# Two channels in one state matmul, and the kernel's spectrum in one part instead of two

## The chip, the cores and the metric

The kernel runs on one core of a Trainium2 chip. A core has five engines that run side by side, each with its own instruction stream: TensorE (PE in the profile; its weight loads are shown as PEld), VectorE (DVE), ScalarE (ACT), GpSimd (POOL) and SyncE (SP). TensorE multiplies a stationary operand, loaded beforehand ("weights"), by a moving one and writes to PSUM; VectorE or ScalarE copy results from PSUM to SBUF, which the text calls an eviction. DMA queues are fed by SP, POOL and ACT. The metric is the time of one execution in microseconds of device time. Three runs of the kernel before gave 386.98, 386.78 and 383.81 us, with the median at 386.78.

## The reference, cut to what matters

Two branches read the same input x (2048 positions, 640 channels) and are mixed by a gate for each position.

```python
g = sigmoid((x * gate_w).sum(-1, keepdims=True))
# A: attention, 32 heads of 20, each position sees 8 positions: itself and 2, 4, ..., 14 back
qkv = x @ wqkv
logits = einsum("bhsd,bhswd->bhsw", q, kg) * Dh ** -0.5      # masked before the start
a = einsum("bhsw,bhswd->bhsd", softmax(logits), vg) @ wo
# B: a long convolution; channel d has 192 complex states n
logdA = dt[:, None] * (A_re + 1j * A_im)
P = exp(logdA[:, :, None] * l[None, None, :])                # l = 0 .. 2047, rounded to bf16
K = einsum("dn,dnl,dn->dl", Cc, P, dt[:, None] * Bc).real    # 640 kernels of 2048 taps
y = irfft(rfft(x, 4096) * rfft(K, 4096))[:2048] + x * Dskip
out = g * a + (1 - g) * y
```

Since l is rounded to bf16, only 641 different values of l occur. The kernel uses this: it computes K at l = 0 and at 20 x 32 values l = 8i + m (i below 32, m out of a list of 20), and takes the spectrum of K by one matrix that has the repeats summed in it.

## The kernel before, in words

**Branch A.** The input is turned (turn), multiplied by wqkv in four pieces of 512 positions (late, L278), and then eight chunks of 256 positions run through products q*k (prod, DVE, L336), a sum over the head (lg, PE, L342), softmax (max, neg, exp, sum, at), a trip through DRAM that spreads the weights (ast, asb, SP), products with the values (pv, DVE, L405), their sums (gat, PE, L411), the eviction (oT), and the multiplication by wo (wo, PE, L429), whose eviction multiplies by g (ga, L438). A chunk's result goes to the DRAM tensor gaS (SP, L448).

**Branch B, the taps.** The 640 channels run in ten chunks of 64. `KGen.plan` gives each chunk 18 argument matmul tasks (arg, PE, L759), whose results ScalarE turns into sines and exponentials (act, L771 and L773). For each of three groups u of states VectorE forms products (pq, three instructions, L790 to L792), and PE sums over the states (kmm, L808). One matmul of a kmm task belongs to one channel: its stationary operand is 32 columns wide (the i), its moving operand 20 columns (the m), and four channels lie side by side in the four column strips of the array. There are 64 such matmuls in a task and four tasks in a chunk (one for u = 0, two for u = 1, one for u = 2), so 2560 matmuls in all. The sums of one chunk lie in one PSUM buffer (slot kb); VectorE evicts it into E (fin, L868).

**Branch B, the spectrum of the taps.** `KSpec.part` works on two parts: the first six chunks (48 columns of 4 channels, 192 in all) and the last four (128 columns). When a part's last chunk is done, PE turns E (move, L885), the result is evicted (kev), and for each of 16 pieces k (8 frequency blocks, real and imaginary) a piece of the spectrum matrix W of 320 KB is fetched (wl, SP, three buffers) and multiplied (ks, L918). The first part does a piece in two tasks, the second in one. Results are evicted to the tile sk (ske, L458 or L460). W is therefore read twice.

**Branch B, the convolution.** The input is fetched a second time (rows), its first transform is 20 tasks (fu, L1029), evicted to Bu (fue). `Conv.spectra` then does, for each part and each of the 8 frequency blocks, the second transform (fp, L1064), its eviction (fe), and six VectorE instructions that multiply by the spectrum (ta, tc, Y, L1091 to L1097). `Conv.inverse` does 20 steps of two tasks (inv, L1122), each evicted to C (cp): twelve belong to the first part and need only its products, eight to the second part. `Conv.tail` does 11 groups of last matmuls (yp, L1164), mixes them with g * a, read from gaS into gaF (gaf, L1144), and stores the result (L1191).

**What sets the order.** Every piece of work is a task with a number, in the order in which `Plan.add` is called. The list SEQ gives the order in which all tasks are emitted and, where a task may run on several engines, the one it runs on (A, D, S, G). Each engine runs its tasks in that order, so a task that waits holds up all that stand behind it on its engine. Buffers are handed over by slots: a task acquires a slot and another releases it. PSUM is divided into two buffers of two banks (slot ar: turns, arg, move, fu, fp), two of one bank (tb: late, gat, wo and ks), one bank for lg and one for kb. For the last eight inverse tasks and the tail, all eight banks become four buffers cy.

Of the kernel before, what the change touches and what calls it, by code (L numbers as in the profile page):

```python
# [50 lines left out]
15A 14S 25 18G 13S 27 16A 20S 12S 23 3A 35 26 30 4A 0A 36A 37A 11S 9S 7S 40 31 8G 10A 24 28 32 29 39 38 49 52 53 44 108 109A 110 111A 106 107A 112 41 113D 104 105A 125  # L51
131 17S 1G 2G 19G 100 103S 101 6G 102S 5S 1158G 252G 124 33 43 126D 132D 54 45 46 135 145 82 136D 146A 63 47 48 50 60D 61D 62 166 127 21 167A 55 128A 137 122 83 138A 123A
141 22A 142A 174 175D 118 51 170 156 116 171A 160 157A 119A 161A 117A 149 150A 120 164 71 165A 68 57 69 70 65 77D 78 79 66 56 1147G 84 73 151 114 139 152A 58 140A 74 177
179 178A 180A 185 88A 186A 183 121A 184A 181 153 86 87 260 89 76 85 90A 182A 64 42 72 59 75 67 187S 91D 92 154A 115A 93 261 133 129 134D 34 95 80 130A 97 98 94 96 81 99
551 253 143 144A 209 262 264 263 265 147 254 210A 148A 162 266 268 267 269 255 270 163A 172 217 256 173A 257 296 218D 271 272 553 555 211 215 554 556 557 558 559 560 273
552 831 561 562 563 564 565 567 566 598 258S 836 597 547G 176 548G 298 212D 216D 274 297 569 568 570 571 299 573 572 574 575 576 300 301 577 302 168 303 579 304 305 169D
578 580 581 582 583 585 584 586 188 587 599 213 588 600 601 603 602 604 306 589 189D 591 214D 275 1156S 155G 331S 276 841 549 550 259G 332 590 605 307 607 592 606 608 609
610 611 612 192 613 158 614 615 617 616 618 593 643 644 219G 619 620 621 623 622 624 625 627 626 628 629 631 630 632 633 634 645 646 594 193D 277 1157 635 280 159D 595
637 596 647 649 648 650 241 651 653 652 654 278 655 657 283 334 279D 636 640 656 658 659 660 661 662 663 664 665 666 667 668 308 638 669 198 639 671 199D 242D 309 670 672
673 674 675 676 310 206 677 679 678 680 641 295G 689 690 311 312 735 736 333 691 681 642 683 336 284 693 682 335 692 694 207A 695 697 696 698 281 282D 285D 338 686 699  # L60
337 701 684 700 702 703 704 200 705 286 707 339 706 708 709 710 287D 201D 288 711 713 289A 712 714 204 715 717 716 685 719 687 718 720 340 368 313 688 727 721 723 205A
722 724 194 725 737 726 738 195A 243 739 741 728 740 742 743 744 244A 290 745 747 341 746 748 292 749 751 750 752 729 732 342 291D 293A 730 731 753 755 754 756 314 757
759 343 315A 758 760 344 208 202 190 761 763 345 316 319 370 191D 762 764 765 767 766 768 346 317 773 318A 769 770 733 369 771 371 782 781 294 347 912 348 911 783 320 772
785 784 786 321A 203A 734 774 372 374 373 787 789 788 790 375 249 376 404 377 791 793 250A 792 794 247 378 379 248A 380 775 795 322 381 324 797 776 796 798 799 800 323D
382 325A 326 801 803 777 802 805 804 405 807 806 808 327A 328 809 811 810 812 329A 196 813 815 220 778 406 408 349 352 814 816 197A 817 913 818 914 407 779 409 915 917
221A 916 350 919 353 410 780 918 920 351A 354A 921 923 411 922 924 245 925 927 926 928 246A 224 929 931 355 412 819 440 367G 820 413 356 821 442 414 824 930 932 225A 933
935 934 936 357A 222 937 939 223A 226 228 415 938 940 251G 957 383 384 330 958 385 941 943 227A 416 942 944 822 823 229A 358 417 945 947 946 948 359A 825 230 418 959 961
360 441 443 231A 960 962 361A 963 965 238 964 966 239A 826 949 444 446 445 448 967 969 362 232 968 970 363A 233A 388 827 447 449 364 828A 365A 450 829 830A 234 451 235A
452 971 973 386 950 236 972 974 387A 975 977 453 403G 240 1148G 976 978 1003 419 1004 420 366 389 979 981 237A 980 982 951 476 391 954 454 478 390D 952 953 983 985 955
984 986 987 988 477 989 990 392 991 479 993 393A 394 992 994 395A 455 1005 1007 396 398 1006 1008 1009 1011 397A 1010 1012 399A 832 1013 1015 480 421 482 995 956 833D 481  # L70
400 1014 1016 1017 1019 1018 1020 483 996 1021 1023 1022 1024 997 1000 484 401A 422 1025 1027 998 999 1026 1028 423A 1029 1031 1030 1032 834 837 485 1001 835A 838A 424
427 1041 1002 1033 1035 839 1034 1036 840A 425 1037 1039 426A 428 842 1038 1040 1049 1051 1052 1149G 1150G 1151G 1152G 1153G 1154G 1155G 1050 456 439G 402 429D 486 430
843A 1053 1055 431A 1054 1056 487 432 434 433A 488 435A 1057 1059 1058 1060 844 436 489 845A 437A 1061 1063 1062 1064 1043 512 457 490 514 846 851 856 491 492 438 475G
1159G 460 1042 847 458 1044 1065 1067 848A 1066 1068 513 515 1045 1069 1071 459A 1070 1072 516 463 849 517 1073 1075 850A 461 464 1074 1076 462A 465A 1161 1162A 466 468
1077 1078 467A 469A 1046 518 520 1047 519 521 1079 1081 1080 1082 470 472 471A 473A 522 1087 1048 523 1083 1085 493 1084 1086 524 852 1163 1165 1088 525 494 1164A 853A
1166A 526 1167 1169 854 1168A 1170A 495A 1089 1092 1171 1173 1172A 857 1174A 1175 1177 858A 1176A 1178A 1160S 474 527 861 528 511G 496 499 497 855D 498A 529 1179 1180A
1181 500 1183 1090 1091 1182A 501D 1184A 1093 502 504 1201 1203 532 503D 505A 506 507A 508 509A 1202D 1204D 1205 1206 1208 1210 1209A 1211A 530 1215 1216A 859 1217 535
1207 531A 860D 1218A 866 510 871 1185 533 1186A 1222 862 1224 1223A 1225A 534D 1212 1094 863D 1213 1214 1219 536 1187 537A 538 540 539A 541A 542 544 543D 545A 1229 1230A
1188A 864 867 865D 1220 1221 868D 1189 1190A 1191 869 1231 872 1192A 870A 1226 1227 873D 1236 1232A 1237A 1193 1194A 546 876 881 874 877 1238 1195 878D 1239A 879 1197
1196D 1199 880D 1228 875A 1233 1234 1198A 1200A 882 884 883A 885D 1235 1097 1095 1096A 1098D 886 891 1357G 1358G 1359G 887 889 888A 1243 890D 1244A 1240 1245 1246A 1241  # L80
1242 892 894 893A 895A 1250 1251A 896 897 898A 899 900A 1247 1248 1249 901 906 902 904 903A 907 905A 908A 909 910D 1254 1099 1102 1105 1100 1101A 1252 1257 1253D 1258D
1103 1104A 1255 1256 1259 1260 1261 1108 1262 1106 1107A 1263A 1109 1110A 1264 1265 1266 1111 1297 1298 1299A 1114 1117 1112 1113A 1267 1268A 1272 1115 1277 1273A 1278A
1118 1116D 1269 1300 1301 1303 1304 1270 1271 1305D 1119A 1120 1123 1126 1302A 1121 1122A 1274 1275 1124 1282 1129 1132 1127 1125A 1283A 1306 1307 1309 1310 1130 1128A
1276 1279 1280 1281 1308A 1311A 1287 1133 1131D 1288A 1134A 1312 1313 1315 1316 1135 1138 1141 1136 1314A 1292 1139 1317A 1137D 1284 1285 1140D 1286 1289 1290 1293A 1318
1319 1321 1322 1144 1142 1145 1320A 1323A 1146A 1324 1325 1326A 1291 1327 1328 1329A 1330 1331 1332A 1143D 1294 1295 1296 1333 1334 1360G 1335D 1361G 1362G 1363G 1364G
1365G 1366G 1367G 1368G 1336 1337 1338A 1339 1340 1341D 1342 1343 1345 1346 1348 1349 1344A 1351 1347D 1350A 1352 1354 1353D 1355 1356A 1369 1370 1372 1373 1371 1374 1375
1376 1379 1384 1380 1377 1385 1381 1378 1382 1383 1386 1391 1394 1398 1387 1388 1389 1390 1392 1395 1393 1396 1397 1399 1400 1401 1402 1403 1405 1406 1404 1407 1408 1410
1411 1409
# [3 lines left out]
class Task:  # L92

    def __init__(self, idx, name, eng, fn, deps, after, acq, rel, table):
        self.idx, self.name, self.engs, self.fn, self.table = idx, name, eng, fn, table
        self.deps, self.after, self.acq, self.rel = [d for d in deps if d], [d for d in after if d], list(acq), list(rel)


class Plan:

    SLOTS = {"ar": 2, "tb": 2, "lg": 1, "kb": 1, "trg": 5, "exq": 5, "pq": 2, "qs": 2, "ks": 2, "vs": 1, "vw": 1, "vc": 2, "prod": 2,
             "at": 2, "asb": 2, "pv": 2, "oT": 1, "ga": 1, "pc": 6, "cy": 4, "yp": 4, "ot": 7, "tt": 4, "W": 3, "su": 3}
# [46 lines left out]
class Attn:  # L149
# [159 lines left out]
    def plan_core(self, pl, pvb, g_sb, ps):  # L309
# [12 lines left out]
        for sc in range(S // C):  # L322
# [10 lines left out]
            for e in range(5):  # L333
# [4 lines left out]
                def logits(_, e=e, b=b):  # L338
                    if e == 0:
                        b["lg"] = ps.tile([128, W, 64], F32, name="lg")  # L340
# [987 lines left out]
```

## Time and profile before

| what | us |
|---|---|
| median of three runs | 386.78 |
| the profiled execution: its own time | 386.59 |
| its span, first to last instruction | 384.8 |
| PE busy | 314.6 |
| DVE busy | 304.5 |
| ACT busy | 293.2 |
| first argument matmul (L759) starts | 66.3 |
| last argument matmul starts | 255.3 |
| last spectrum matmul (L918) ends | 356.2 |

The profile gives the busy time of each engine, the stretches in which it was idle and what ended them ("<-PE ar L759" is the matmul of line 759 that writes ar; "issue" is time in which the engine waited for nothing that the profile shows). A line of a helper stands for all its callers: L458 and L460 are the evictions by ScalarE and VectorE. The busy time of PE is counted from the start of each matmul to its modelled end, which overlaps the next one; a distance between two starts is therefore the better price.

### The profile page before, as it was taken

The page shows a single profiled execution, that of the slowest core. Times are in us where ns is not written, and L with a number is a line of the kernel's source. Part 1 is how long each engine was busy: PE and PEld are TensorE (multiplying, and loading weights), DVE is VectorE, ACT ScalarE, POOL GpSimd, SP SyncE. Part 2 cuts the span into 40 slices and gives each one's busy share as a digit, 9 for nine tenths or more (in the row PEclk, how much of TensorE's full clock was granted, in tenths as well). Part 3 has the DMA queues.
Part 4 walks back from the last instruction along what each step waited for, and adds up shares of the span by engine and source line. Part 5 has one row for each costly group of instructions (what it writes and reads, how often), then busy time and mean ns, then how long its engine had stood idle before and what let it go on. Part 6 is the DMA issues. An engine that isn't in the chain of part 4 may idle for free. (4 is left out here: it accounts for less than half of the span.)

```text
span 384.8 us, 14995 instructions
## 1 busy us (share of the span) xinstructions
PE 314.6 (82%) x6666; PEld 209.9 (55%) x6686; DVE 304.5 (79%) x429; ACT 293.2 (76%) x445; POOL 59.3 (15%) x95
## 2 busy tenths in 40 slices
PE   0289998797869999998985989889799956999750
PEld 0255563343325554545442666559688955999740
DVE  4969998689658999998993979849597754896881
ACT  3599995899759999999893989678376632687690
POOL 8510024300210010012250020100002220000032
PEclk9999999899789999999996999989899998999896
DMA  8973157866123124136399263514023898664046
GB/s 277 382 186 104 52 168 104 207 120 167 42 48 68 32 79 91 35 90 155 70 223 177 77 144 91 136 63 112 4 70 112 315 211 206 181 174 130 3 105 172
DMA packets 47786, 49.86 MB, mean 130 GB/s; under 512 B 29016, under 2 KB 37754, under 8 KB 47722
## 3 DMA queue, kind: packets, MB, share of 16 engines
q1 hardware_dynamic: 40234, 28.17, 29.0%
q0 software_dynamic: 5280, 18.08, 19.5%
q10 hardware_dynamic: 2208, 2.65, 1.9%
q8 instruction: 52, 0.85, 0.9%
q14 instruction: 12, 0.10, 0.1%
HBM read 37.00 MB, written 11.89 MB: 127 GB/s over the span
## 5 line engine op out<-in xcount | busy, mean ns | idle before, releaser
L771 ACT ACTIVATE big<-ar 128x576 bf16<-128x576 int16 x120 | 71.1, 657 | 12.7 <-PE ar L759 12.3
L278 PE MATMUL tb<-bufA 128*128 128x512 bf16 x280 | 74.0, 396 | 4.7 <-issue 1.3
L759 PE MATMUL ar<-Rarg,L 64*128 64x288 bf16 (+1 forms) x480 | 51.0, 280 | 16.3 <-issue 8.8
L918 PE MATMUL tb<-KE,W 128*64 128x192 bf16 (+1 forms) x1280 | 53.5, 236 | 9.6 <-DMA W<-c_spec 7.3
L918 PEld LDWEIGHTS <-W 128*64 128x64 bf16 x1280 | 47.0, 111 | 11.9 <-DMA W<-c_spec 8.7
L773 ACT ACTIVATE big<-ar 128x832 bf16<-128x832 f32 x60 | 48.6, 873 | 6.2 <-PE ar L759 6.0
L278 PEld LDWEIGHTS <-bufA 128*128 128x128 bf16 x300 | 33.1, 121 | 34.1 <-issue 13.1
L405 DVE TENSOR_TENSOR pv<-vc,asb 128x4096 bf16<-128x4096 bf16 (+1 forms) x24 | 45.9, 1927 | 3.8 <-PE tb L411 2.8
L759 PEld LDWEIGHTS <-L 64*128 64x128 bf16 x480 | 19.7, 94 | 49.8 <-issue 45.5
L458 ACT ACTIVATE bufA<-tb 128x384 bf16<-128x384 f32 (+1 forms) x31 | 16.8, 541 | 20.0 <-PE tb L918 19.8
L429 PE MATMUL tb<-wo_sb,oT 128*128 128x320 bf16 x160 | 28.5, 322 | 2.7 <-ACT ga L438 2.7
L336 DVE TENSOR_TENSOR prod<-qk 128x2048 bf16<-128x2048 bf16 x20 | 24.1, 1217 | 6.6 <-PE lg L342 6.6
L808 PE MATMUL kps<-tbx 128*32 128x20 bf16 (+1 forms) x2560 | 26.1, 175 | 3.5 <-issue 3.5
L808 PEld LDWEIGHTS <-tbx 128*32 128x32 bf16 (+1 forms) x2560 | 22.8, 92 | 10.5 <-issue 8.4
L336 DVE TENSOR_TENSOR prod<-uga 128x2048 bf16<-128x2048 bf16 x20 | 24.1, 1220 | 2.5 <-PE lg L342 2.1
L438 ACT ACTIVATE ga<-tb,g_sb 128x320 bf16<-128x320 f32 x27 | 14.4, 537 | 13.5 <-PE tb L429 9.2
L330 POOL DMA_DIRECT2D vc<-vS x14 | 10.1, 737 | 93.7 <-DVE pv L405 91.7
L792 DVE TENSOR_TENSOR tbx<-big 128x1280 bf16<-128x1280 bf16 x30 | 24.5, 816 | 0.0
L411 PE MATMUL tb<-pv,ind 128*64 128x512 bf16 (+1 forms) x192 | 22.6, 361 | 0.1
L458 ACT ACTIVATE big<-ar 128x1024 bf16<-128x1024 f32 x19 | 18.9, 1023 | 4.3 <-PE ar L1029 4.1
L185 PE MATMUL ar<-ident,uga 128*128 128x128 bf16 x80 | 7.9, 264 | 17.4 <-DMA ident<-c_ident 16.9
L429 PEld LDWEIGHTS <-oT 128*128 128x128 bf16 x160 | 14.8, 103 | 11.9 <-issue 4.7
(170 smaller groups left out, 561.3 us busy)
## 6 DMA issues: line engine op xcount, KB each, us to landing
W<-c_spec SPq DMA_DIRECT2D x32, 320.0 KB, 3.6
vc<-vS POOLq DMA_DIRECT2D x14, 327.5 KB, 5.9
Sprm<-pc SPq DMA_DIRECT2D x12, 240.0 KB, 3.7
L<-Sprm SPq DMA_DIRECT2D x80, 36.0 KB, 2.4
gaS<-ga SPq DMA_DIRECT2D x8, 320.0 KB, 3.9
uga<-in_A_x_dram POOLq DMA_DIRECT2D x8, 320.0 KB, 9.0
uga<-gaS POOLq DMA_DIRECT2D x8, 320.0 KB, 10.2
asb<-aS SPq DMA_DIRECT2D x16, 128.0 KB, 3.6
```

Source lines behind the costliest of these rows:

```text
L278: nc.tensor.matmul(ppf, self.wq[:, kt, which * D + e:(which + 1) * D:5], self.xT[:, c0 // 1024, kt, c0 % 1024:c0 % 1024 + SC], start=(kt = ...
L336: nc.vector.tensor_tensor(b[e][:], self.part(ch, 0)[:, e, o:o + C].unsqueeze(1).to_broadcast([128, W, C]), win(self.part(ch, 1)[:, e, :], ...
L405: nc.vector.tensor_tensor(b["pv", e][:, 0:2 * n], taps, aw, ALU.mult)
L411: nc.tensor.matmul(b["op", e][64 * a:64 * a + 64, 0:n, :], self.twin, b["pv", e][:, a:2 * n:2, w, :], start=(w == 0), stop=(w == HV - 1), ...
L429: nc.tensor.matmul(apf[:, :320], b["oT"][:, e, i * 128:(i + 1) * 128], wo_sb[:, e, hf * 320:(hf + 1) * 320], start=(e == 0), stop=(e == 4))
L458: nc.scalar.activation(o, i, ACT.Identity)
L759: nc.tensor.matmul(ar[:, g2, a0:a0 + ncol], L[rows, sb, gp, l0:l0 + 128], R[rows, c0:c0 + ncol], start=True, stop=True, tile_position=(64 ...
L771: nc.scalar.activation(dst[:, 2 * gp:2 * gp + 2, sub, :], ar[:].bitcast(I16)[:, :, 0:2 * SW:2], ACT.Sin, scale=SCL)
L773: nc.scalar.activation(dst[:, 2 * gp:2 * gp + 2].rearrange("p g s n -> p g (s n)"), ar[:, :, 0:2 * EW], ACT.Exp)
L792: nc.vector.tensor_tensor(qq[:, :, :, :], trg[:, :, KI:].rearrange("p a (v m) -> p a v m", v=2), exq[:, :, KI:].unsqueeze(2).to_broadcast( ...
L808: nc.tensor.matmul(kps[32 * g:32 * g + 32, h, NM * ql:NM * ql + NM], pt[rows, k, v, :], qq[rows, k, v, :], start=(g not in started), stop= ...
L918: nc.tensor.matmul(kp[64 * c:64 * c + 64, fl], wt, ke.rearrange("p x g -> p (x g)"), start=(m == first and fl == 0), stop=(m == M5 - 1), s ...
```

## The change

**The state matmul.** Two channels now share one matmul: the stationary operand holds the 32 columns of each of two channels, the moving operand the 20 columns of each. The result is 64 x 40, of which the two diagonal blocks of 32 x 20 are used. Two column strips of 64 are used instead of four of 32. A task has 32 matmuls, so there are 1280. A chunk is evicted in two halves h (fin on VectorE or ScalarE, 20 tasks in place of 10), each out of a PSUM buffer of its own turn of the one slot kb. The tables are laid out so that two channels' columns lie side by side; `move` picks the diagonal blocks.

**The spectrum in one part.** E holds five chunks at a time, is turned into KE twice, and after the last chunk 32 tasks do the whole spectrum with 320 columns (80 columns of 4 channels). W is read once, in 32 pieces of 160 KB with four buffers. The real pieces use slot ar, the imaginary ones a buffer kp of two banks that takes the place of lg and kb. The second transform and the products run over all 320 columns; the products of the last frequency block are cut in four. All 20 inverse tasks come after the products (task cb needs blocks 0 to 6 and slice cb // 5 of block 7) and use cy. There are two buffers su in place of three.

**Smaller edits.** gaS is stored as two halves of 320 channels, with two DMAs for each chunk, and gaF is read from it in the order j = k % 4, half k // 4. The direct tap at l = 0 is fetched straight into KD (no copy kdp).

**The order.** SEQ is new for all 1390 tasks. Up to the last argument matmul the branch-A work of PE ends at wo3 and gat4 (before: wo5 and gat5), no spectrum task stands there (before: eight of the first part), and two fu tasks (before: one). On SP the fetches wl4 to wl7 stand behind the store gaS5, wl8 behind gaS6 and wl12 behind gaS7; the fetches psi1, gaf3, gaf4, gaf5 and gaf7 stand behind the last wl.

```diff
-    SLOTS = {..., "kb": 1, ... "W": 3, "su": 3}
+    SLOTS = {..., "kb": 1, "kp": 1, ... "W": 4, "su": 2}
...
-                def kmm(_, u=u, b=b, j=0):
-                    if u == 0 and j == 0:
-                        b["kps"] = pk.tile([128, 2, 256], F32, name="kps", tag="kb")
+                def kmm(_, u=u, b=b, h=0):
+                    if u == 0 or (u == 1 and h):
+                        b["started"] = set()
+                        b["kps"] = pk.tile([128, 512], F32, name="kps", tag="kb")
...
-                        for ql in range(4 * j, 4 * j + 4) if u == 1 else range(8):
-                            for h in (0, 1) if u == 1 else (u // 2,):
-                                for g in range(4):
-                                    r0 = 64 * (g // 2) if u == 1 else 0
...
-                                    nc.tensor.matmul(kps[32 * g:32 * g + 32, h, NM * ql:NM * ql + NM],
-                                                     pt[rows, k, v, :], qq[rows, k, v, :],
+                        for ql in range(8):
+                            for w in range(2):
+                                r0 = 64 * w if u == 1 else 0
...
+                                k = 4 * ql + 2 * ((w + h) % 2)
+                                nc.tensor.matmul(kps[64 * w:64 * w + 64, 2 * NM * ql:2 * NM * ql + 2 * NM],
+                                                 pt[rows, v, k:k + 2, :].rearrange("p a n -> p (a n)"), qq[rows, k:k + 2, v, :],
...
+            evict(nc, en, self.E[:, :, h, :, CQ * cl:CQ * cl + CQ].rearrange("p m a q -> p q a m"), b["kps"][:, 0:2 * NM * CQ].rearrange("p (q a m) -> p q a m", a=2, m=NM))
+        return pl.add(f"fin{c}{h}", "AD", fn, deps=[m] + (self.moved if c == NHF and not h else []), after=fins[-1:], rel=[("kb", m0)])
...
+    def spectrum(self, pl, ps, sk, opened, free, ends):
+        for k in range(32):
+            i, ro = divmod(k, 2)
...
+                queue(nc, e).dma_start(w["t"][:].rearrange("p f m x -> p (f m x)"), self.w_d[k])
+            ld = pl.add(f"wl{k}", "S", load, deps=self.past, after=[ld], acq=["W"])
...
+                kp = b["kp"] = ps[ro]().tile([128, 2, 512], F32, name=("ar", "kp")[ro])
+                first = -1 if ro == 0 else 0
+                for m in range(first, M5):
+                    for fl in range(2):
+                        for c in range(2):
+                            wt = self.one[:] if m < 0 else w["t"][:, fl, m, :]
+                            ke = self.KD[:, c] if m < 0 else self.KE[:, m, c]
+                            nc.tensor.matmul(kp[64 * c:64 * c + 64, fl, 0:320], wt, ke.rearrange("p g x -> p (g x)"),
+                                             start=(m == first), stop=(m == M5 - 1), skip_group_check=True, tile_position=(0, 64 * c))
...
+            m = pl.add(f"ks{ro}x{i}", "P", spec, deps=[ld, self.kd] + self.kevs + (ends if ro else []), after=[prev], acq=[tag], rel=[("W", ld)])
...
+            for hf in range(2):
+                for r in range(2):
...
+                    m = prev = pl.add(f"fp{fb}{hf}{r}", "P", spec, deps=fues + [self.phis[fb]], after=[prev] + kg.lastkmm, acq=["ar"])
+                    v = pl.add(f"fe{fb}{hf}{r}", "AD", move, ...)
...
+            np_ = 4 if fb == 7 else 1
+            for z in range(np_):
+                x = slice(320 // np_ * z, 320 // np_ * (z + 1))
...
-                prev = pl.add(f"inv{cb}{ro}", "P", inv, deps=[self.muls[p, fb] for fb in range(8)] + ..., acq=[("ar", "cy")[p]] if ro == 0 else [])
+                prev = pl.add(f"inv{cb}{ro}", "P", inv, deps=[self.muls[fb, 0] for fb in range(7)] + [self.muls[7, cb // 5]], ..., acq=["cy"] if ro == 0 else [])
...
-                nc.sync.dma_start(self.gaS[c0:c0 + C].rearrange("(i p) d -> p i d", p=128), b["ga"][:])
+                for h in range(2):
+                    nc.sync.dma_start(self.gaS[h, c0:c0 + C].rearrange("(i p) d -> p i d", p=128), b["ga"][:, :, 320 * h:320 * h + 320])
```

More of the change, by code (lines that the diff above doesn't have):

```diff
@@ L476 @@
 EW = 4 * (KI + NM)
-PARTS = ((0, 6), (6, 10))
+NHF = NCH // 2
 NF = 4096
@@ L1232, in opened @@
             kg.open(now["big"], now["tbx"])
-            cv.open(now["big"], now["tbx"])
             ksp.open(ctx.enter_context(tc.tile_pool(name="kk", side="right", bufs=1)))
+            cv.open(now["big"], now["tbx"], ksp.E)
     def space():
@@ L1242, in space, with pair @@
         return now
+    def pair():
+        if "kp" not in now:
+            cK.close()
+            now["kp"] = cP.enter_context(tc.tile_pool(name="kp", bufs=1, space=PSUM))
+        return now["kp"]
     def banks():
```

348 lines of the change are left out of this document (151 added, 197 removed).

## The prediction

> **What bounds the kernel now.** I read the page's first part, then cut the span at the marks of the time table and asked for the busy time of each engine in each stretch (the last row is a part of the second stretch).
>
> ```profile
> span 384.8 us, 14995 instructions
> 0.00:66.30 66.30, 46.10 (x332) 26.57 (x336) 54.37 (x67) 50.99 (x66) 21.18 (x37) 1.00 0.65 180
> 66.30:255.30 189.00, 164.52 (x3599) 88.86 (x3616) 161.06 (x203) 163.05 (x259) 25.06 (x37) 0.94 0.47 106
> 255.30:356.20 100.90, 91.22 (x2310) 83.10 (x2308) 71.34 (x130) 62.82 (x91) 7.36 (x12) 0.97 0.55 150
> 356.20:384.80 28.60, 12.78 (x433) 11.35 (x432) 17.70 (x31) 16.30 (x29) 5.66 (x10) 0.82 0.37 94
> 120.00:200.00 80.00, 76.45 (x1660) 40.22 (x1668) 76.72 (x97) 76.89 (x126) 13.09 (x20) 1.00 0.42 92
> ```
>
> After the stretch's length come PE, PEld, DVE, ACT and POOL. From the first to the last argument matmul (the "tap stretch", 189.0 us) PE, DVE and ACT have nearly the same work, 161 to 165 us, so no engine alone is the bound; in 80 us of it all three are 96% busy. The 100.9 us after it (the "spectrum stretch") belong to PE: 91 busy, DVE 71, ACT 63. The last 28.6 us (the "tail") are a chain.
>
> Next, where PE stands still: its timeline, the waits of ACT and PE, the DMA issues.
>
> ```profile
> 110.92 0.35 PE L759 MATMUL ar<-Rarg,L 64*128 64x208 bf16 x4 [3.25 <-issue]
> 206.31 0.42 PE L759 MATMUL ar<-Rarg,L 64*128 64x288 bf16 x2 [5.51 <-issue]
> 274.97 0.46 PE L808 MATMUL kps<-tbx 128*32 128x20 bf16 x40 [2.18 <-issue]
> ACT big L771 <- PE ar L759: 12.3, 17, 5.3
> PE tb L918 <- DMA W<-c_spec: 7.3, 4, 4.0
> W<-c_spec SPq DMA_DIRECT2D x32, 320.0 KB, 3.6
> uga<-gaS POOLq DMA_DIRECT2D x8, 320.0 KB, 10.2
> ```
>
> Three holes of 10.9 us end with "issue", beside or inside a run of kmm matmuls; ACT waits 12.3 us for arguments, once for 5.3 us, which is the second hole. In the spectrum stretch PE waits 7.3 us for W. What feeds PE its instructions may be read from the queues and the counts:
>
> ```profile
> PE 314.6 (82%) x6666; PEld 209.9 (55%) x6686; DVE 304.5 (79%) x429; ACT 293.2 (76%) x445; POOL 59.3 (15%) x95
> q8 instruction: 52, 0.85, 0.9%
> ```
>
> 0.85 MB for 6666 + 6686 instructions are 64 bytes each, 52 packets of 16 KB, or 256 instructions a packet. One kmm task is 128 of them, so two tasks use up a packet in 1.3 us. I take the holes for PE running dry; the page doesn't show it.
>
> **The state matmul.** Rows by line:
>
> ```profile
> L808 PE MATMUL kps<-tbx 128*32 128x20 bf16 (+1 forms) x2560 | 26.1, 175 | 3.5 <-issue 3.5
> L808 PEld LDWEIGHTS <-tbx 128*32 128x32 bf16 (+1 forms) x2560 | 22.8, 92 | 10.5 <-issue 8.4
> L1064 PEld LDWEIGHTS <-L 128*64 128x64 bf16 x256 | 10.0, 112 | 1.4 <-issue 1.0
> 337.59 0.39 PE L918 MATMUL tb<-KD,one 128*64 128x128 bf16 x8
> 337.82 1.28 PE L918 MATMUL tb<-KE,W 128*64 128x128 bf16 x40
> ```
>
> A task of 64 takes 26.1 / 40 = 0.65 us, of which the loads fill 0.57 (8.9 ns each), 36 ns for a set of four strips. No row has 64 columns of weights with 40 moving. Low bound: half the instructions at 8.9 ns, 0.28 + 0.08 = 0.36 us. High bound: a pair in two strips with 128 moving columns, (1.28 - 0.39) / 16 pairs = 56 ns; 16 pairs and 0.08 make 0.98 us. A load of 64 columns takes 20 ns longer than one of 32, and 36 ns is the nearest pace: 0.6 us. So PE's time for these hardly changes; the instructions halve, 2560 fewer. [...]
>
> Each half's buffer is now handed over in mid-chunk: the second task of u = 1 waits until fin has evicted the first. Behind it on PE stand argument tasks, and ACT waits for those. The list puts two to eleven other PE tasks between, 0.6 us or more, against a fin of 0.48 us (below); I cost it at 0, with up to 0.5 us x 10 in the range.
>
> **The spectrum.** Distances of two runs of each width give the price of a pair:
>
> ```profile
> 285.89 0.99 PE L918 MATMUL tb<-KE,W 128*64 128x192 bf16 x20
> 298.96 1.83 PE L918 MATMUL tb<-KE,W 128*64 128x192 bf16 x40
> ```
>
> (1.83 - 0.99) / 10 = 84 ns for 192 columns, 56 for 128; 320 columns by the first rate are 140 ns. Before: 352 pairs of each, 29.6 + 19.7 = 49.3 us. After: 352 x 140 = 49.3. Nothing is gained on PE but 1408 instructions. W's bytes halve to 5.2 MB, and gaF is read in runs of 16 rows instead of single rows of 640 bytes. Fetch k+4 may start when ks k is done, three tasks (4.5 us) ahead, against 3.6 us to landing for twice the size. But wl4, wl8 and wl12 stand behind stores of gaS on SP, and gaF still moves 2.6 MB. I leave 2.0 of the 7.3 us (bounds 0 and 7.3).
>
> **What ACT and DVE do.**
>
> ```profile
> L458 ACT ACTIVATE bufA<-tb 128x384 bf16<-128x384 f32 x20 | 10.2, 509 | 11.7 <-PE tb L918 11.6
> L460 DVE CAST bufA<-tb 128x384 bf16<-128x384 f32 x12 | 6.6, 551 | 6.4 <-PE tb L918 6.4
> L458 ACT ACTIVATE KE<-ar 128x640 bf16<-128x640 f32 x1 | 0.7, 704 | 0.8 <-PE ar L885 0.8
> L460 DVE CAST KE<-ar 128x640 bf16<-128x640 f32 x1 | 0.8, 815 | 0.0
> L868 DVE CAST E<-kps 128x320 bf16<-128x320 f32 x10 | 4.8, 484 | 2.4 <-PE kps L808 2.4
> L792 DVE TENSOR_TENSOR tbx<-big 128x1280 bf16<-128x1280 bf16 x30 | 24.5, 816 | 0.0
> L1091 DVE TENSOR_TENSOR tbx<-tbx,bufA 128x768 bf16<-128x768 bf16 (+1 forms) x32 | 14.5, 484 | 7.6 <-ACT bufA L458 7.4
> L438 ACT ACTIVATE ga<-tb,g_sb 128x320 bf16<-128x320 f32 x27 | 14.4, 537 | 13.5 <-PE tb L429 9.2
> L405 DVE TENSOR_TENSOR pv<-vc,asb 128x4096 bf16<-128x4096 bf16 (+1 forms) x24 | 45.9, 1927 | 3.8 <-PE tb L411 2.8
> ```
>
> 48 spectrum evictions become 32 of 640 columns (0.70 or 0.82 us), some 3 us less; 96 products at 0.484 us (46.5) become 42 of 1280 elements at 0.816 and 24 of 320 at about 0.32 (slope of the two rows), 41.9 in all. Ten more fins cost 4.8. All that is on engines with room in the spectrum stretch.
>
> **The three stretches.** The new list takes PE work out of the tap stretch and puts it into the next:
>
> ```profile
> L918 PE MATMUL tb<-KE,W 128*64 128x192 bf16 x160 | 8.2, 247 | 2.1 <-issue 2.1
> 288.44 3.04 PE L429 MATMUL tb<-wo_sb,oT 128*128 128x320 bf16 x20
> 284.53 1.03 PE L411 MATMUL tb<-pv,ind 128*64 128x512 bf16 x8
> L1029 PE MATMUL ar<-F1c,uga 128*64 128x128 bf16 x320 | 20.0, 274 | 0.0
> ```
>
> Eight spectrum tasks (first row, with their 16 direct taps 88 pairs x 84 ns = 7.4 us), eight wo tasks (0.76 each, 6.1), three gat (2.4), less one fu (1.0): 14.9 us. With them go 19 evictions at some 0.54 us and two pv at 1.9, 14.1 us of DVE and ACT; nine more fins come in, 4.4. So the tap stretch has PE 164.5 - 14.9 - 1.9 = 147.7, ACT and DVE 4.8 less each, 158.2 and 156.3. Bounds: ACT at the packing of 120 to 200 us (96.1%) gives 164.6 us, at that of the whole stretch (86.3%) 183.4. ACT's idle time was 26.0 us; with PE 10 us below the others and half the kmm instructions I drop the 12.3 it waited for arguments: 158.2 + 13.7 = 171.9, **17.1 less**.
>
> Spectrum stretch: 100.9 + 14.9 - 5.3 (W) - 1.1 (half of the hole at 274.97) - 5.3 for ten inverse steps that move to the tail (two take 1.07, below) = 104.1, **3.2 more**.
>
> ```profile
> 339.03 1.07 PE L1122 MATMUL ar<-GAB,bufA 64*128 64x128 bf16 x32
> 356.82 2.85 ACT L458 ACTIVATE C<-ar 128x1024 bf16<-128x1024 f32 x3
> 360.52 2.56 DVE L460 CAST C<-cy 128x1024 bf16<-128x1024 f32 x2 [0.57 <-PE cy L1122]
> 364.31 1.94 ACT L458 ACTIVATE C<-cy 128x1024 bf16<-128x1024 f32 x2 [0.57 <-PE cy L1122]
> ```
>
> Tail: after the last spectrum task two evictions on ACT (1.4) and four products of 320 (1.3), with hand-overs 3.2 us until the first inverse. Then 20 evictions of C: 13 on ACT at 0.95 (12.4); DVE first has 18 products (5.4), then 7 at 1.28 (9.0). The last ends some 14.5 us on. From there the rest is unchanged: 366.25 to 384.8, 18.5. Sum 36.2, **7.6 more**; PE is no longer what ends last there, the evictions are.
>
> The start I leave at 0, within 3 us. Sum: -17.1 + 3.2 + 7.6 = -6.3, span 378.5. The profiled execution took 386.59, 1.8 beyond its span: **380.3 us**. Its time is 0.2 below the median, so both may be compared directly.
>
> **The rivals.**
>
> *The overlap is lost* (the slower side). Place: PE in the spectrum stretch, where work that lay beside ACT's now ends last. If the holes are not PE running dry, or DVE and ACT hold each other up, the tap stretch stays at 86.3%, 183.4 us: span 390.0, time 391.8. It decides as soon as the tap stretch gives back less than the 10.8 us that the others take. For it: ACT and DVE were as busy as PE there. Against: ACT's waits name PE. [...]
>
> *The tap stretch packs fully*, 164.6: span 371.2, time 373.0. For it: the 80 us at 96%; against: the start of the stretch and the DRAM trip of the softmax weights are not touched.
>
> *The state matmul gets dearer*, 0.98 us: 37 tasks in the stretch cost 12.2 us more, PE is at 161.8 and binds again, the stretch some 187 us: time 395. [...] Against: 36 ns for four loads.
>
> *W still comes late*, behind the stores on SP: 5.3 us more, 385.6.
>
> **Chances.** Forecast (376 to 386) 0.42, overlap lost 0.20, full packing 0.18, W late 0.12, dear matmul 0.08. The measurement tells about 1% (3.9 us) from no change. Faster: 0.18 and 0.33 of the forecast, 0.51. Same: 0.09 and 0.12, 0.21. Slower: 0.28. Range 371 to 394: it takes in full packing and the lost overlap, and leaves the dear matmul out.
>
> **What would show it.** Right: the last argument matmul near 238 us, holes with "issue" in kmm runs under 5 us, a kmm task of 0.5 to 0.7 us, W waits under 3 us, and 35 to 37 us after the last spectrum matmul. Wrong: PE idle in the tap stretch with ACT and DVE still 86% busy; PE waiting for fin at L808; a tail beyond 40 us.

## The result, and the profile after

The changed kernel takes 440.4 us (439.46 to 442.48) beside 386.9 us (383.81 to 387.15) of the kernel before: a ratio of 1.141, 95% interval 1.134 to 1.148. I had forecast 380.3 us, with 371 to 394 as the range. It is slower by 54 us.

First the page's first part after, and the stretches, cut at the same marks as before: first and last argument matmul (now L758), end of the last spectrum matmul (now L912).

```profile
span 439.0 us, 10744 instructions
PE 326.6 (74%) x4553; PEld 216.3 (49%) x4574; DVE 336.0 (77%) x414; ACT 353.6 (81%) x424; POOL 51.2 (12%) x89
q8 instruction: 35, 0.57, 0.6%
...
0.00:69.26 69.26, 45.90 (x337) 27.29 (x343) 55.62 (x69) 49.70 (x65) 19.59 (x36) 1.00 0.53 166
69.26:254.24 184.98, 153.82 (x2217) 81.40 (x2230) 159.56 (x199) 167.76 (x247) 22.31 (x37) 0.91 0.44 92
254.24:400.24 146.00, 107.85 (x1424) 91.17 (x1424) 95.54 (x97) 109.64 (x79) 3.63 (x7) 0.94 0.35 90
400.24:439.04 38.80, 19.03 (x585) 16.40 (x580) 25.31 (x50) 26.51 (x37) 5.66 (x10) 0.82 0.27 69
```

The instructions fell as the change says, by 4251. But ACT and DVE, which do fewer operations than before (424 instead of 445, 414 instead of 429), are busy 60 and 32 us longer. ACT was to have 158 us of work in the tap stretch and has 167.8; in the spectrum stretch it has 109.6 and is the busiest engine, where before it had 62.8. That stretch takes 146.0 us instead of the 104.1 forecast, and even ACT is busy in only 75% of it.

Fewer operations that take longer: the next view is the groups of operations, different shapes kept apart.

```profile
L457 ACT ACTIVATE bufA<-ar 128x640 bf16<-128x640 f32 x14 | 44.5, 3214 | 3.6 <-PE ar L912 3.6
L457 ACT ACTIVATE bufA<-kp 128x640 bf16<-128x640 f32 x11 | 34.9, 3173 | 8.0 <-PE kp L912 8.0
L459 DVE CAST bufA<-kp 128x640 bf16<-128x640 f32 x5 | 15.2, 3031 | 3.5 <-PE kp L912 3.5
L459 DVE CAST bufA<-ar 128x640 bf16<-128x640 f32 x2 | 6.0, 2994 | 0.6 <-PE ar L912 0.6
L457 ACT ACTIVATE E<-kps 128x320 bf16<-128x320 f32 x15 | 24.1, 1609 | 0.6 <-PE kps L807 0.6
L459 DVE CAST E<-kps 128x320 bf16<-128x320 f32 x5 | 7.8, 1555 | 1.1 <-PE kps L807 1.1
L457 ACT ACTIVATE KE<-ar 128x800 bf16<-128x800 f32 x4 | 3.2, 835 | 0.5 <-PE ar L881 0.5
L457 ACT ACTIVATE tbx<-ar 128x640 bf16<-128x640 f32 x19 | 15.9, 842 | 8.4 <-PE ar L1055 6.5 <-ACT bufA L457 1.8
L459 DVE CAST tbx<-ar 128x640 bf16<-128x640 f32 x13 | 10.6, 821 | 19.5 <-PE ar L1055 19.4
```

The first four rows are the 32 spectrum evictions: 100.6 us, at 3.0 to 3.2 us each, where I had counted 0.70 and 0.82. The next two are the 20 fins: 31.9 us, at 1.6 us each, where I had counted 0.48. The last three rows move as many elements or more, from PSUM to bf16 like the others, and take 0.82 to 0.84 us. So neither the number of elements nor the types make the difference. The rows don't show the addresses; the code does. Both dear groups write one 2-byte element, then step 256 bytes (x in sk, L916) or 320 bytes (m in E, L864); the cheap ones write runs of two neighbours (tbx) or 40 (KE). In the kernel before, the same two operations wrote f or q innermost, that is 2 or 4, or 8, neighbours at a time.

The waits fit that (what waited, for what, us in total, times, longest; the last row is the group of the loads that bring W into the array):

```profile
PE ar L1055 <- ACT bufA L457: 17.5, 8, 4.4
DVE E L1074 <- ACT bufA L457: 16.6, 7, 7.4
PE kp L912 <- ACT bufA L457: 5.7, 5, 2.2
...
PE kps L807 <- DVE E L459: 8.6, 1, 8.6
...
L912 PEld LDWEIGHTS <-W 128*64 128x64 bf16 x640 | 47.1, 120 | 11.4 <-issue 8.5 <-DMA W<-c_spec 0.7
```

Three of the rows name the spectrum eviction on ACT. The fourth is one stop of PE for a fin in the tap stretch, to which the experiments come back. In the last row the wait for W is down to 0.7 us, and no row of PE's matmuls names W any more (7.3 us before).

**Theory**: the two write orders make the loss, on either engine, and the rest of the prediction holds. **Rivals**: the new order of tasks lost the overlap; the evictions are slow only beside other work, or because of the PSUM banks that they read; the hand-over of the state matmul's buffer holds PE whatever fin costs.

### The profile page after: what moved, and what is told of

Same layout as the page of the kernel before. It is cut to its first block, busy times and chain, and to the rows that moved or that the text cites. A ratio compares the mean times of both kernels' runs of the same rounds, so it can differ in the third digit from the quotient of the medians.

```text
span 439.0 us, 10744 instructions
## 1 busy us (share of the span) xinstructions
PE 326.6 (74%) x4553; PEld 216.3 (49%) x4574; DVE 336.0 (77%) x414; ACT 353.6 (81%) x424; POOL 51.2 (12%) x89
## 3 DMA queue, kind: packets, MB, share of 16 engines
q1 hardware_dynamic: 44458, 24.90, 24.1%
## 5 line engine op out<-in xcount | busy, mean ns | idle before, releaser
L758 PE MATMUL ar<-Rarg,L 64*128 64x288 bf16 (+1 forms) x480 | 55.6, 286 | 18.6 <-ACT big L772 8.8
L457 ACT ACTIVATE bufA<-ar 128x640 bf16<-128x640 f32 (+1 forms) x23 | 53.5, 2355 | 9.2 <-PE ar L184 5.6
L912 PEld LDWEIGHTS <-W 128*64 128x64 bf16 x640 | 47.1, 120 | 11.4 <-issue 8.5
L758 PEld LDWEIGHTS <-L 64*128 64x128 bf16 x480 | 21.5, 95 | 55.0 <-issue 49.7
L457 ACT ACTIVATE bufA<-kp 128x640 bf16<-128x640 f32 x11 | 34.9, 3173 | 8.0 <-PE kp L912 8.0
L807 PE MATMUL kps<-tbx 64*64 64x40 bf16 (+1 forms) x1280 | 28.5, 189 | 9.8 <-DVE E L459 8.6
L912 PE MATMUL kp<-KE,W 128*64 128x320 bf16 x320 | 28.8, 330 | 7.5 <-ACT bufA L457 5.7
L807 PEld LDWEIGHTS <-tbx 64*64 64x64 bf16 (+1 forms) x1280 | 25.2, 115 | 17.6 <-issue 14.9
L1055 PE MATMUL ar<-big,L 128*64 128x320 bf16 x128 | 14.9, 317 | 23.2 <-ACT bufA L457 17.5
L912 PE MATMUL ar<-KE,W 128*64 128x320 bf16 x320 | 27.1, 318 | 0.0
L334 DVE TENSOR_TENSOR prod<-qk 128x2048 bf16<-128x2048 bf16 x20 | 24.1, 1228 | 3.5 <-PE lg L340 2.1
L1074 DVE TENSOR_TENSOR E<-tbx,bufA 128x1280 bf16<-128x1280 bf16 (+1 forms) x22 | 13.9, 656 | 16.6 <-ACT bufA L457 16.6
L459 DVE CAST tbx<-ar 128x640 bf16<-128x640 f32 x13 | 10.6, 821 | 19.5 <-PE ar L1055 19.4
L457 ACT ACTIVATE E<-kps 128x320 bf16<-128x320 f32 x15 | 24.1, 1609 | 0.6 <-PE kps L807 0.6
L791 DVE TENSOR_TENSOR tbx<-big 128x1280 bf16<-128x1280 bf16 x30 | 24.4, 815 | 0.0
```

The costliest lines, as they stand in the source:

```text
L334: nc.vector.tensor_tensor(b[e][:], self.part(ch, 0)[:, e, o:o + C].unsqueeze(1).to_broadcast([128, W, C]), win(self.part(ch, 1)[:, e, :], ...
L457: nc.scalar.activation(o, i, ACT.Identity)
L459: nc.vector.tensor_copy(o, i)
L758: nc.tensor.matmul(ar[:, g2, a0:a0 + ncol], L[rows, sb, gp, l0:l0 + 128], R[rows, c0:c0 + ncol], start=True, stop=True, tile_position=(64 ...
L791: nc.vector.tensor_tensor(qq[:, :, :, :], trg[:, :, KI:].rearrange("p a (v m) -> p a v m", v=2), exq[:, :, KI:].unsqueeze(2).to_broadcast( ...
L807: nc.tensor.matmul(kps[64 * w:64 * w + 64, 2 * NM * ql:2 * NM * ql + 2 * NM], pt[rows, v, k:k + 2, :].rearrange("p a n -> p (a n)"), qq[ro ...
```

## The experiments

### The write orders, each alone and both

Edits of the changed kernel. The same bytes go to the same places; only the order in which one instruction walks over them differs. The experiments ran in three groups, each with the kernel before beside it, and its median was 384.18, 384.92 and 383.69 us there (these three runs are the first group), against 386.88 beside the changed kernel: a difference taken across groups is good to some 3 us, and a ratio is always to the kernel before of the same group.

```diff
 # spectrum eviction, L916
-sk[:, ro, :, 2 * i:2 * i + 2].rearrange("p (x g) f -> p f g x", g=4), b["kp"][:, :, 0:320].rearrange("p f (g x) -> p f g x", g=4)
+sk[:, ro, :, 2 * i:2 * i + 2].rearrange("p (x g) f -> p g x f", g=4), b["kp"][:, :, 0:320].rearrange("p f (g x) -> p g x f", g=4)
 # fin, L864
-self.E[...].rearrange("p m a q -> p q a m"), b["kps"][...].rearrange("p (q a m) -> p q a m", a=2, m=NM)
+self.E[...].rearrange("p m a q -> p a m q"), b["kps"][...].rearrange("p (q a m) -> p a m q", a=2, m=NM)
```

The spectrum eviction alone:

> The changed kernel with the spectrum evictions written in pairs: f innermost, then x, then g; the same bytes to the same places. Theory: an eviction costs 0.75 to 1.0 us instead of 3.0 to 3.2, the 32 of them about 28 us instead of 101; the spectrum stretch falls from 146 us to 105 to 115, the time to 400 to 412 us. Rival (the new order of tasks lost the overlap, the evictions are slow beside it): above 430 us with PE idle for other reasons.

Measured: 397.4 us (396.75 to 400.15), 43.0 less than the changed kernel and below the range that was expected. Fin alone:

> The changed kernel with fin written with q innermost, eight contiguous elements; the same bytes to the same places. Theory: a fin costs about 0.5 us instead of 1.6, 20 of them 22 us less on ACT and DVE, 19 of them in the tap stretch where these two are the bound: 8 to 12 us off, 428 to 433 us. Rival (the hand-over of the state matmul's buffer holds PE, whatever fin costs): within 3 us of 440.

Measured: 423.5 us (421.45 to 426.49), 16.9 less, where 8 to 12 were expected. So fin's price counts, and not only the hand-over behind it. Both:

> Both edits. Theory (the two write orders are nearly the whole of what went wrong): 384 to 398 us, the tap stretch 172 to 178 us and the spectrum stretch 103 to 112. Rival (something else of the change costs as much, the order of tasks or the state matmul): above 405 us.

Measured: 380.35 us (379.61 to 382.51), a ratio to the kernel before of 0.990 (0.985 to 0.995): better than the 384 to 398 that were expected, and about 1% faster than the kernel before. The two gains add up, 59.9 of 60.05 us. The groups of this kernel:

```profile
L457 ACT ACTIVATE bufA<-ar 128x640 bf16<-128x640 f32 x14 | 10.5, 749 | 14.2 <-PE ar L912 14.2
L457 ACT ACTIVATE bufA<-kp 128x640 bf16<-128x640 f32 x11 | 8.2, 741 | 7.0 <-PE kp L912 7.0
L459 DVE CAST bufA<-kp 128x640 bf16<-128x640 f32 x5 | 4.1, 819 | 0.4 <-PE kp L912 0.4
L459 DVE CAST bufA<-ar 128x640 bf16<-128x640 f32 x2 | 1.6, 822 | 2.9 <-PE ar L912 2.9
L457 ACT ACTIVATE E<-kps 128x320 bf16<-128x320 f32 x15 | 6.9, 460 | 0.0
L459 DVE CAST E<-kps 128x320 bf16<-128x320 f32 x5 | 2.4, 485 | 1.0 <-PE kps L807 1.0
```

24.4 us for the spectrum evictions, 9.3 for the fins: 98.8 us less on two engines. By the prediction's prices they would be 23.2 (25 x 0.70 + 7 x 0.82) and 9.7. Its stretches:

```profile
0.00:68.93 68.93, 44.77 (x338) 26.22 (x344) 55.63 (x69) 49.61 (x65) 19.59 (x36) 1.00 0.54 166
68.93:237.53 168.60, 150.03 (x2215) 79.71 (x2230) 153.19 (x197) 154.51 (x247) 23.02 (x37) 0.93 0.49 101
237.53:342.59 105.06, 97.80 (x1426) 82.10 (x1425) 81.13 (x99) 55.66 (x79) 4.26 (x8) 0.97 0.46 119
342.59:377.94 35.35, 17.89 (x584) 15.62 (x580) 25.13 (x50) 22.56 (x37) 5.66 (x10) 0.85 0.37 94
```

The order of tasks in this kernel is the changed kernel's, so the lost overlap falls as the cause of the 60 us. Where each order hurt, the marks in the traces of the two single edits tell: with fin alone mended the last argument matmul starts at 238.8 us instead of 254.2, and the spectrum stretch still takes 147.0; with the spectrum eviction alone mended it starts at 253.1, and the spectrum stretch takes 106.4. So a fin costs in the tap stretch, where ACT had the most work: its 15 fins became 17.2 us shorter (24.1 to 6.9 with both edits), the stretch 15.3 with fin alone.

### The kernel before, with the write order of the change

```diff
-evict(nc, en, sk[:, ro, 32 * c0:32 * c1, ...], b["v"].rearrange("p f x -> p x f"))
+evict(nc, en, sk[:, ro, 32 * c0:32 * c1, ...].rearrange("p x f -> p f x"), b["v"])
-nc.vector.tensor_copy(e[...], b["kps"][...].rearrange("p c (q m) -> p c m q", m=NM))
+nc.vector.tensor_copy(e[...].rearrange("p c m q -> p c q m"), b["kps"][...].rearrange("p c (q m) -> p c q m", m=NM))
```

> The kernel before with its spectrum evictions and its fin written element by element (x innermost, 64 bytes apart, instead of f; m innermost instead of q), everything else as it was. Theory: 4.9 ns an element, 384 elements 1.9 us and 512 elements 2.5 us, fin 1.6 us: 85 us more on ACT and DVE, a third of it in the tap stretch, and the time 412 to 432 us. Rival (the write order only hurts together with the new order of tasks or the one-part spectrum): within 8 us of the kernel before.

Measured: 419.6 us (419.42 to 420.15), a ratio of 1.089 (1.083 to 1.094), inside the range that was expected. Groups of this kernel:

```profile
L458 ACT ACTIVATE bufA<-tb 128x384 bf16<-128x384 f32 x20 | 37.1, 1942 | 5.0 <-PE tb L918 4.9
...
L868 DVE CAST E<-kps 128x320 bf16<-128x320 f32 x10 | 16.9, 1689 | 2.6 <-PE kps L808 2.5
```

The 509 ns of before are 1942, the 484 of fin 1689. The write order alone costs the kernel before some 35 us, with its own order of tasks, its two parts and its own state matmul. 64 bytes from element to element (the spectrum eviction here) are as dear as the 256 of the changed kernel: 5.1 ns an element, 1942 for 384, beside 5.0, 3214 for 640.

### The evictions by themselves

A kernel with nothing but evictions, the engines one after the other. (It and the second one below ran once each; their figures are means of four and of three records of that execution.) Three of its lines:

```python
A(lane(o, 2), p4)      # 320 elements, 2 bytes apart; then 4, 8, ... 512
A(sk[:, :, :, 0:2].rearrange("p x g f -> p f g x"), kv)                                   # as in the changed kernel
A(sk[:, :, :, 0:2].rearrange("p x g f -> p g x f"), kv.rearrange("p f g x -> p g x f"))   # pairs
```

> A kernel of evictions alone, nothing of the reference is computed: 320 elements from PSUM to bf16 in SBUF as four runs of 80, with 2, 4, 8, 16, 32, 64, 128, 256, 320 and 512 bytes from one element to the next, on ACT and on DVE; the 640 elements of a spectrum eviction in three orders (x innermost as in the changed kernel, pairs f innermost in steps of 256 bytes, the same pairs in steps of 64 bytes); fp32 instead of bf16 results 256 bytes apart; bf16 from SBUF instead of PSUM, scattered; a scattered read with a dense result. Theory (the dear thing is the single 2-byte write that steps far): 0.4 to 0.5 us at 2 bytes, near 1.6 us at 256 and 320 bytes on both engines, with the step somewhere between 8 and 64 bytes; 3.0 to 3.2 us for the spectrum eviction as it stands, 0.75 to 1.0 us for both orders in pairs; from SBUF as dear as from PSUM. Rival 1 (the two PSUM banks are read in an unlucky order): the stride makes no difference at 320 elements, the spectrum orders differ. Rival 2 (evictions were slow only because the other engines ran beside them): all rows 0.4 to 0.9 us here, where nothing runs beside.

Measured, ns for 320 elements by the bytes from one to the next:

| bytes apart | 2 | 4 | 8 | 16 | 32 | 64 | 128 | 256 | 320 | 512 |
|---|---|---|---|---|---|---|---|---|---|---|
| ACT | 437 | 525 | 876 | 1583 | 1504 | 1557 | 1592 | 1592 | 1556 | 1592 |
| DVE | 492 | 514 | 866 | 1572 | 1492 | 1545 | 1580 | 1579 | 1545 | 1580 |

Groups on DVE (the spectrum order as in the changed kernel, then pairs 256 and 64 bytes apart, fp32 results 256 bytes apart, and single bf16 elements 256 bytes apart out of SBUF):

```profile
L72 DVE CAST o<-kp 128x640 bf16<-128x640 f32 x4 | 12.0, 2999 | 29.3 <-ACT o L38 29.3
L73 DVE CAST o<-kp 128x640 bf16<-128x640 f32 x4 | 3.3, 825 | 0.1
L74 DVE CAST o<-kp 128x640 bf16<-128x640 f32 x4 | 3.3, 824 | 0.1
L75 DVE COPY w<-kp 128x320 f32<-128x320 f32 x4 | 2.7, 686 | 0.0
L76 DVE COPY o<-src 128x320 bf16<-128x320 bf16 x4 | 3.8, 950 | 0.0
```

ACT gave 3010, 704, 704, 698 and 1629 for these five. A scattered read (256 bytes apart) with a dense result took 737 ns on ACT and 516 on DVE. So both rivals fall: with nothing beside them the evictions take 3.0 us as in the kernel, and the price is there with one PSUM bank (1592 and 1579 ns at 256 bytes) or out of SBUF (1629 and 950). It is full at 16 bytes (1583 and 1572 ns, then 1492 to 1592) and not at 8 (876 and 866). One part of the expectation missed: out of SBUF the scattered write costs DVE 950 ns, not as much as out of PSUM.

A second such kernel asked what the unit is, with groups of neighbours and with fp32:

> Evictions alone again, 320 elements from PSUM each, on ACT and DVE, nothing of the reference is computed: bf16 results in groups of 1, 2, 4, 8 and 16 neighbours that start every 64 bytes; groups of 2 that begin at an odd element, across a 4-byte border; fp32 results 4, 8, 16 and 64 bytes apart; single bf16 results 64 bytes apart from fp32 in SBUF. Theory (what is dear is an element that is alone in its 4 bytes): 1.5 us for single ones, 0.45 to 0.55 us for every group from 2 up, near 1.5 us for pairs across the border, fp32 at 0.45 to 0.7 us whatever the distance. [...]

Measured, ns for 320 elements (bf16 groups start every 64 bytes):

| | single | 2 | 2, odd start | 4 | 8 | 16 | fp32 4 B apart | 8 | 16 | 64 |
|---|---|---|---|---|---|---|---|---|---|---|
| ACT | 1559 | 439 | 864 | 437 | 437 | 437 | 434 | 774 | 733 | 708 |
| DVE | 1524 | 492 | 852 | 492 | 491 | 491 | 480 | 690 | 719 | 692 |

Two of these groups on DVE, the pairs (L71) and the pairs with an odd start (L72):

```profile
L71 DVE CAST o<-kp 128x320 bf16<-128x320 f32 x3 | 1.5, 492 | 0.1
L72 DVE CAST o<-kp 128x320 bf16<-128x320 f32 x3 | 2.6, 852 | 0.1
```

The theory doesn't hold as a whole. Groups from two up are at the dense price, as it said (437 to 439 and 491 to 492 ns); but a pair across a 4-byte border goes only some 35 to 40% of the way up, on both engines (864 and 852). Lone fp32 elements cost 0.21 to 0.34 us above dense ones, lone bf16 elements 1.0 to 1.1 us; 16 bytes apart, bf16 at 1583 and 1572 (first table) is twice as dear as fp32 at 733 and 719. Single bf16 out of fp32 in SBUF, 64 bytes apart, took 1592 ns on ACT and 852 on DVE. Why a lone 2-byte element costs more than a lone 4-byte one stays open.

One pattern runs through the bf16 rows out of PSUM whose elements stand alone: from 4 to 16 bytes apart the price rises with the distance, from 525 and 514 ns (ACT and DVE) at 4 bytes to 876 and 866 at 8 and 1583 and 1572 at 16, about 88 ns for each byte more, and beyond 16 bytes it doesn't rise (1492 to 1592). The pairs with an odd start cost about as much as single elements 8 bytes apart, 864 and 852. Even pairs (439 and 492) and fp32 (774 and 690 at 8 bytes, 733 and 719 at 16) don't follow it. What causes it no run shows.

### What is left: the hand-over, and W

With both write orders mended, two stops of PE remain that the prediction had at 0 and at 2.0 us. The first, in the timelines of PE and of DVE of the changed kernel:

```profile
101.76 1.04 PE L807 MATMUL kps<-tbx 64*64 64x40 bf16 x32 [8.61 <-DVE E L459]
...
96.02 2.29 DVE L403 TENSOR_TENSOR pv<-vc,asb 128x4096 bf16<-128x4096 bf16 x1 [8.74 <-DMA asb<-aS]
98.23 0.68 DVE L789 TENSOR_TENSOR tbx<-big 128x1024 bf16<-128x1024 bf16 x1
...
100.17 1.53 DVE L459 CAST E<-kps 128x320 bf16<-128x320 f32 x1
```

The second half's first task (kmm of u = 1) waits for the first fin; that fin stands on DVE behind a product that waits 8.7 us for its softmax weights to come back from DRAM. First the fin to ACT (592D becomes 592A in the list):

> Both write orders mended, and the first fin taken from DVE, where it stands behind a product that waits for the softmax weights, to ACT. Theory: the 6.7 us in which PE stands before the second task of the first chunk go, and 3 to 6 us of the time with them, 374 to 378 us. Rival (DVE and ACT make it up elsewhere, or the wait only moves to the product): within 2 us of 380.3.

Measured: 378.1 us (377.54 to 379.08), some 2.2 us less, just above the expected range and across two groups of runs. The wait moved as the rival says: PE now stops 4.2 us for the products of the same chunk (L791), which stand behind the same product. So the product itself was moved back in DVE's list, from ahead of the chunk's last products to behind the first fin and two more operations:

> Both write orders mended, and on DVE the first product with the softmax weights put behind the last product of the first chunk, the first fin and two more operations that are ready earlier; PE's order is as it was. Theory (that product waits some 8 us for its weights to come back from DRAM, and everything behind it with it): PE's stop before the second or third task of the first chunk goes altogether, 4 to 7 us of the time, 373 to 376 us. Rival (the product itself is what the rest waits for, and DVE's idle time is only moved): within 2 us of the 378.1 us that the fin on ACT gave.

Measured: 373.65 us (373.25 to 375.88), 6.7 us less than with the write orders alone. PE's stop is gone, and the "issue" row of the state matmul's loads falls with it from 10.9 us, 6.6 the longest, to 5.5; in the waits of that kernel:

```profile
PEld L807 <- issue: 5.5, 21, 0.5
ACT big L770 <- PE ar L758: 5.7, 14, 1.6
PE ar L912 <- DMA W<-c_spec: 4.6, 1, 4.6
```

The second is the last row: PE waits once for W, in the middle of the spectrum stretch. On SP that load stands behind the last store of gaS. Two loads of W moved ahead of it:

> Both write orders mended, and the loads of W for the spectrum tasks 12 and 13 put ahead of the last store of gaS on SP, where they stood behind it. Theory: the one wait of PE for W, 4.5 us, goes, and 3 to 5 us of the time with it, 375 to 378 us. Rival (what makes W late is the traffic of gaF and psi that starts at the same time, not its place): the wait stays over 3 us or comes two tasks later, and the time within 2 us of 380.3.

Measured: 381.1 us (380.32 to 385.6), a ratio of 0.995 (0.990 to 1.000): nothing gained. The wait came two and three tasks later, in two pieces, as the rival says:

```profile
PE kp L912 <- DMA W<-c_spec: 3.6, 1, 3.6
PE ar L912 <- DMA W<-c_spec: 2.1, 1, 2.1
```

So its place on SP was not the cause. The two loads were not even issued earlier (294.3 and 296.0 us, before the edit 294.2 and 295.8): the matmuls that free their buffers came no sooner. What moved was the store, from 292.0 to 296.4 us, and the wait moved with it. The stretches around it, of the kernel with both orders mended, show another (the DMA share is the last column but one):

```profile
294.00:298.00 4.00, 4.00 (x62) 3.35 (x60) 3.83 (x6) 2.37 (x4) 2.95 (x6) 1.00 0.67 173
298.00:302.00 4.00, 4.00 (x64) 3.35 (x62) 2.91 (x5) 2.79 (x5) 0.69 (x2) 1.00 1.07 285
302.00:306.00 4.00, 1.08 (x16) 0.65 (x12) 3.50 (x5) 1.02 (x2) 0.00 (x0) 1.00 0.95 217
```

The store's end lets POOL issue four loads of gaF and three of psi from 294.6 to 298.7 us, and the DMA share goes from 0.67 to 1.07 and 0.95. The five loads of W issued from 295.8 to 302.6 us landed after 4.0 to 11.2 us; the four issued from 280 to 287 us and the next one, at 310.5, after 2.2 to 2.3. Four loads of gaF taken from POOL and spread over SP (1339, 1340, 1341 and 1345 in the list):

> Both write orders mended, and the four loads of gaF that POOL issues all at once after the last store of gaS put on SP, one behind each second load of W from the twenty-second on. Theory (what makes W late is the transfers of gaF and psi beside it): the wait for W falls from 4.5 us to under 2, the time by 3 to 5 us to 375 to 378. Rival (psi alone fills the DMA engines, or gaF then comes too late for the tail): within 2 us of 380.3 or above.

Measured: 376.0 us (375.32 to 377.65), 4.4 us less than with the write orders alone; the wait fell from 4.5 us to 2.1, nearly as far as expected. What psi has to do with the rest was not tested. Both moves:

> Both write orders mended, the product moved and the loads of gaF moved. Theory: the two gains add up, 369 to 373 us. Rival (one of them only moves its wait): 374 to 380 us.

Measured: 369.3 us (367.54 to 369.48), a ratio to the kernel before of 0.960 (0.956 to 0.964). The two gains add up (6.7 and 4.4, 11.0 together). Neither move belongs to the change that was forecast.

## Why the prediction was wrong, point by point

The stretches in us (the last row is the median, the forecast's last row its own figure):

| | before | forecast | changed | write orders mended |
|---|---|---|---|---|
| to the first argument matmul | 66.3 | 66.3 | 69.3 | 68.9 |
| tap stretch | 189.0 | 171.9 | 185.0 | 168.6 |
| spectrum stretch | 100.9 | 104.1 | 146.0 | 105.1 |
| tail | 28.6 | 36.2 | 38.8 | 35.4 |
| span | 384.8 | 378.5 | 439.0 | 377.9 |
| time | 386.9 | 380.3 | 440.4 | 380.35 |

**The step that failed** is in "What ACT and DVE do": "48 spectrum evictions become 32 of 640 columns (0.70 or 0.82 us)" and "ten more fins cost 4.8". I took these prices from rows with the same shape and types, the KE eviction and the old fin, and not from rows with the same write pattern. The diff shows the pattern: f and q, which stood innermost, moved outward. The terms measured 3.0 to 3.2 and 1.6 us. They put 92 us on ACT and DVE together (353.6 and 336.0 us busy against 282.3 and 315.1 with the orders mended), and 60 us on the time. I gave this no bounds, since I took the operations as known; none of my rivals has this mechanism, and the range could not hold it.

**"On engines with room in the spectrum stretch"** fell with it: ACT got 109.6 us of work there instead of 55.7.

**The tap stretch** comes out near the forecast once the fin is priced right: 168.6 us, ACT 154.5 us busy (forecast 158.2) and 14.1 idle (13.7), the last argument matmul at 237.5 us (238). That the idle time agrees is luck. "I drop the 12.3 it waited for arguments" failed: ACT still waits 12.1 us for them, once for 7.4 us, beside PE's stop at the hand-over, and of the 13.7 us that were to stay some 2 are left. The row with the write orders mended:

```profile
ACT big L770 <- PE ar L758: 12.1, 15, 7.4
```

With the product moved these waits are 5.7 us and the stretch is 162.0 (68.8 to 230.8 us). That is what the rival "the tap stretch packs fully" had: 164.6, and 373.0 us for the time, where 373.65 was measured.

**The spectrum stretch and the tail** come near too: 105.1 and 35.4, forecast 104.1 and 36.2. Inside them the wait for W was 4.5 us, not 2.0; in the changed kernel as it stands it is 0.7, since PE came later than W. With gaF moved the wait is 2.1 us and the stretch 100.0, so the rest of it was forecast some 4 us too long.

**The total** with the orders mended agrees with the forecast within 0.1 us, and that is luck in good part. The start was 2.6 us longer than I left it, the tap stretch 3.3 shorter, and two stops of PE, priced at 0 and 2.0 us, fill what the stretches were forecast too long. And the kernel before took 384.18 us beside it, not 386.6: the gain is 3.8 us, where 6.3 was forecast.

**The state matmul** takes 28.8 / 40 = 0.72 us a task (rows below), not 0.60, within the bounds. These 5 us of PE need not show in the time, since PE has 18.6 us idle in that stretch with the orders mended (168.6 less 150.0); no run tested it.

```profile
L807 PE MATMUL kps<-tbx 128*64 128x40 bf16 x640 | 14.8, 192 | 1.2 <-ACT E L457 1.2
L807 PE MATMUL kps<-tbx 64*64 64x40 bf16 x640 | 14.0, 186 | 8.6 <-DVE E L459 8.6
```

**The hand-over in mid-chunk**, "I cost it at 0, with up to 0.5 us x 10": I looked at what PE has between, and not at what stands ahead of fin on DVE. It is one stop of 8.6 us, 6.7 with the orders mended, beyond the 5 us of the range, and moving the product was worth 6.7 us of the time. "PE waiting for fin", a sign of being wrong, did come.

**The "issue" holes** of 2 to 5.5 us are gone: 35 packets of instructions instead of 52, and no row of PE's matmuls in the changed kernel ends with "issue" for more than 0.5 us. The kernel before with the scattered writes, which differs from it in these writes alone (52 packets there), keeps all three, though ACT and DVE have 78 us more work there; its waits:

```profile
PE ar L759 <- issue: 8.1, 2, 5.1
PE kps L808 <- issue: 3.6, 2, 2.5
```

So the holes go with the list of instructions and not with the evictions. That agrees with PE having run dry; no run tested it by itself.

## What to carry to other kernels

Price an operation from a row with the same innermost write step, not only the same shape and types (here 3.0 to 3.2 us stood against 0.70 and 0.82); the groups of a profile don't show it, so read the access pattern in the code, above all where a change of layout moves a short dimension outward. If a bf16 result must be scattered, leave at least two neighbours innermost, the first at an even element: here that made a spectrum eviction about four times cheaper without moving a byte elsewhere (3214 to 749 ns on ACT, 3031 to 819 on DVE), and pairs with an odd start took 864 and 852 ns where even ones took 439 and 492. And before a wait is costed at nothing, look at what stands ahead of the releasing instruction on its own engine. A total that agrees shows little until its stages have been compared term by term: here two terms of the tap stretch, each over 11 us off, made up for each other.

## What the runs showed of the hardware

- 320 lone bf16 elements written to SBUF from PSUM took 1504 to 1592 ns on ACT and 1492 to 1580 on DVE with 16 bytes and more from one to the next, 4.7 to 5.0 ns each; dense or in even groups of two and more, 437 to 439 and 491 to 492 ns. Pairs with an odd start are in between on both engines, at 864 and 852 ns.
- Lone fp32 elements cost less than half of that (698 and 686 ns for 320 from PSUM at 256 bytes, against 1592 and 1579).
- DVE writes lone elements faster from SBUF (852 ns from fp32 at 64 bytes, 950 from bf16 at 256) than from PSUM (1524 and 1545 at 64, 1579 at 256); ACT doesn't (1592 and 1629 against 1557 to 1559 and 1592).
- Loads of 160 KB that took 2.3 us to land in the median took up to 11.2 us while the DMA engines were full (a share of 0.95 to 1.07 in the rows above).
